# A RetNet layer and a SwiGLU layer on one core: a new order of work, rms_g spread by a product, two row groups transposed by DMA

## Chip, core and metric

One core of one Trainium2 chip. The metric is the device time of one execution in microseconds; each version is run several times and the median counts.

## What is computed

The first half is a recurrent attention with a decaying state, for 4 batches, 8 heads, 768 positions and a head size of 64. The second half normalises each of the 3072 rows of 512, and puts it through a gated layer of width 1536.

```python
for t in range(S):                       # S = 768
    state = gamma * state + k[:, :, t] (outer) v[:, :, t]
    y[:, :, t] = scale * (q[:, :, t] @ state)
x = y.transpose(0, 2, 1, 3).reshape(3072, 512)
xn = x / sqrt(mean(x * x, axis=-1) + 1e-6) * rms_g
g = xn @ w_gate                          # 512 x 1536
out = (g / (1 + exp(-g)) * (xn @ w_val)) @ w_out
```

## The kernel before, in words

The sequence is cut in six chunks (c = 0 to 5) of 128 positions; a chunk has four rows (b = 0 to 3, one for each batch) of 128 positions by 512 columns. Within a chunk the recurrence is done as masked products, and the state carries the rest to the next chunk.

No loop sets the order of work. A string, `ORDER`, lists some 870 steps; each engine runs its own steps strictly in the order of the list, and the waits between engines follow from the data. A step is written name.arguments@engine/banks. The engine letters are D (VectorE), A (ScalarE), P (GpSimd) and S (SyncE, which issues transfers alone). The number behind the slash is one of the eight PSUM banks; a step that writes a bank waits until what was in it has been read.

The steps, with c and b as their first arguments:

- `Lq`, `Lk`, `Lv`: a load of a row of q, k or v (256 KB in float32). GpSimd's loads of q and k turn the values to bfloat16 on the way; rows loaded by SyncE are turned by `Cq` (for c > 0 with a factor) and `Ck`. Loads of chunk 2 wait for the last part of w_out. The buffers are rings (qf, kf: 4, vf: 6, qb: 6, kb: 8).
- `wg`, `wv`, `wo`: a load of some of the twelve 128-wide parts of w_gate, w_val, w_out, all issued by GpSimd.
- `Tq`, `Tk` with `Eq`, `Ek`: a transpose on TensorE into a bank, and its copy to SBUF; from chunk 2 on `tq`, `tk` do both by a DMA transpose, issued by SyncE.
- `A` (scores into two banks a row), `M0`, `M1` (the mask, VectorE), `V` (v times its decay), `Y` (y into a bank), `K` and `U` (the chunk's addition to the state), `B` (state to bfloat16, GpSimd).
- `x` (chunk 1 only, y times its decay), `S` (sum of squares, ScalarE), `R` (1/rms, two GpSimd instructions), `N` (x times 1/rms times rms_g, VectorE).
- `X` with `XE`: the transpose of xn on TensorE and its copy to SBUF; `XE` on SyncE is a DMA transpose in place of both.
- `g`, `v` (c, first and last part, first and last row): gate and value products of the FFN, four matmuls a part; `s` (silu, ScalarE, a ring of 3), `h` (their product, VectorE). In chunk 0 they are cut by rows, so that they can start with the first rows and parts.
- `d`, `e`: the output products, `o` their copy to SBUF (a ring of 4), `st` the store.
- `hot.n`: n matmuls of ones whose result nobody reads. `iota`, `ident`, `causal`: masks made on GpSimd; `vd`, `yd`, `mk0`, `mk1`: decays and masks on ScalarE; `tab`: one silu of one column, which loads ScalarE's table; `rms`: the load of rms_g.

The setup ahead of the list puts a few memsets on VectorE, among them those of the bfloat16 states and of `causal`, which the step `causal` then masks. In the list before, the first steps of GpSimd are `ident`, two loads, `iota`, four loads and parts of the weights; `causal` comes in chunk 0's FFN. `rms` reads rms_g's 512 values once for each of the 128 partitions.

Of the kernel before, what the change touches and what calls it, by code (L numbers as in the profile page):

```python
# [27 lines left out]
g.0.4.5.0.3/4 N.0.3 Ek.1.0@A Tq.1.0/2 wv.9.12 s.0.4.5.0.3 X.0.3/1 Eq.1.0@D K.0.2/0 s.0.5.6.0.3 K.0.1/3 XE.0.3@D
A.1.0/42 g.0.4.6.3.4/5 wv.6.9 M0.1.0 g.0.0.4.3.4/1 U.0.2@A U.0.1@A h.0.5.6.0.3 v.0.4.6.3.4/4 M1.1.0
g.0.8.9.0.4/0 s.0.4.6.3.4 h.0.4.5.0.3 v.0.0.4.3.4/3 s.0.0.4.3.4 Lk.1.1@P g.0.7.8.0.4/7 wg.9.12 V.1.0@D Tk.1.2/2  # L30
g.0.6.7.0.4/5 B.0.2 s.0.8.9.0.4 h.0.4.6.3.4 B.0.1 Y.1.0/6 v.0.11.12.0.4/1 Ek.1.2@A Lq.1.2@P h.0.0.4.3.4 K.1.0/0
# [6 lines left out]
d.0.1.4.8 V.1.2@P M0.1.3 d.0.3.4.8 M0.1.2 V.1.3@P M1.1.3 K.1.2/5 Y.1.2/0 U.1.2@D X.1.1/4 Y.1.3/6 x.1.2 XE.1.1@A
B.1.2 K.1.3/5 d.0.2.4.8 x.1.3 S.1.2 U.1.3@D Lq.2.0@S S.1.3 d.0.0.8.12 R.1.2 Lk.2.0@S d.0.2.8.12 Lv.2.0@S R.1.3
N.1.2 o.0.0@A st.0.0@S d.0.1.8.12 B.1.3 N.1.3 o.0.2@A Lq.2.1@S X.1.2/4 X.1.3/0 o.0.1@A d.0.3.8.12 XE.1.2@D  # L40
Cq.2.0@P XE.1.3@A Lk.2.1@S K.1.1/6 g.1.3.4.0.4/5 o.0.3@A U.1.1@D Ck.2.0@P tq.2.0 v.1.1.2.0.4/3 B.1.1 s.1.3.4.0.4
g.1.0.1.0.4/1 st.0.3@S V.2.0@P st.0.2@S g.1.6.7.0.4/2 s.1.0.1.0.4 Lv.2.1@S tk.2.0 Cq.2.1@P g.1.1.2.0.4/4
s.1.6.7.0.4 v.1.3.4.0.4/0 Lq.2.2@S Ck.2.1@P tq.2.1 g.1.2.3.0.4/7 h.1.3.4.0.4 g.1.9.10.0.4/6 s.1.1.2.0.4 st.0.1@S
h.1.1.2.0.4 tk.2.1 v.1.0.1.0.4/5 g.1.11.12.0.4/1 V.2.1@P Lk.2.2@S h.1.0.1.0.4 v.1.7.8.0.4/2 s.1.2.3.0.4 Lv.2.2@S
v.1.2.3.0.4/0 Cq.2.2@P v.1.6.7.0.4/4 h.1.2.3.0.4 tq.2.2 v.1.8.9.0.4/3 h.1.6.7.0.4 v.1.9.10.0.4/5 Lq.2.3@S
s.1.9.10.0.4 s.1.11.12.0.4 g.1.8.9.0.4/7 Ck.2.2@P h.1.9.10.0.4 Lk.2.3@S g.1.4.5.0.4/0 tk.2.2 s.1.8.9.0.4 V.2.2@P
A.2.0/4615 h.1.8.9.0.4 s.1.4.5.0.4 v.1.10.11.0.4/7 Lv.2.3@S M1.2.1 M0.2.1 K.2.1/3 Cq.2.3@P v.1.5.6.0.4/0 M0.2.0
# [474 lines left out]
```

## Time and profile before

| | |
|---|---|
| median of 3 runs | 239.07 us (238.51 to 240.12) |
| the profiled execution, first to last instruction | 236.7 us |
| last TensorE matmul ends | 233.76 us |
| granted TensorE clock | 1.000 |
| filler matmuls (hot_ps) | 121, 10.7 us busy |
| ScalarE copies, last one ends | 234.06 us |
| data moved | 34.89 MB, mean 147 GB/s |

The profiled execution has no time of its own apart from its span; the median stands 2.4 us above that span. Times in the profile count from the span's start. TensorE's busy time includes the fillers, and the ends of matmuls are modelled.

Rows that are used below, from the views by line and by tile (one instruction each unless said otherwise):

| what | engine | us |
|---|---|---|
| mask on scores, am<-a_ps 128x512 | VectorE | 0.68 |
| silu times value, hT, 128x512 | VectorE | 0.68 |
| x<-y_ps, st_f addition | VectorE | 0.69 |
| xn, 128x512 | VectorE | 0.75 |
| kT, qT, xnT copies, 128x512 bf16 | VectorE / ScalarE | 0.42 / 0.59 |
| kb from kf, 128x512 | GpSimd / ScalarE | 0.61 / 0.62 |
| vp from vf, 128x512 | GpSimd / VectorE / ScalarE (8 parts) | 1.04 / 0.69 / 2.02 |
| qb from qf, 128x512 | GpSimd | 1.04 |
| sum of squares, with the read of its result | ScalarE | 0.80 |
| 1/rms, two instructions | GpSimd | 0.75 |
| table load for silu | ScalarE | 1.28 |
| DMA transpose of xn, issue / issue to landing | SyncE | 1.22 / 2.5 |
| store of a row, issue to landing | SyncE | 2.0 late in the run |

### The profile page before, as it was taken

The numbers are of one execution on the slowest core, as the hardware profiler recorded it, in microseconds if no ns is written. First come the engines' busy times: TensorE is split into PE (matmuls) and PEld (weight loads), VectorE is DVE, ScalarE is ACT, GpSimd is POOL, SyncE is SP. The second block draws the span as 40 slices with busy tenths as digits, with TensorE's granted clock in tenths as the row PEclk, the third lists the DMA queues.
The fourth block names the chain that finished last, engine by engine and source line by source line (L and its number), as shares of the span: only waits on it lengthen the run. The fifth ranks groups of instructions, "written<-read, shape, count | busy, mean of one in ns | idle before, by whom it ended". The sixth has DMA issues, their size and how long they took to land.

```text
span 236.7 us, 4515 instructions
## 1 busy us (share of the span) xinstructions
PE 227.5 (96%) x1729; PEld 123.5 (52%) x1729; DVE 121.1 (51%) x212; ACT 87.7 (37%) x187; POOL 109.5 (46%) x182
## 2 busy tenths in 40 slices
PE   8889999989999999899999999999999999999995
...
GB/s 142 206 208 160 149 206 188 126 209 130 235 231 210 191 195 154 194 248 123 39 233 171 179 204 158 198 138 141 215 216 74 0 25 95 38 47 0 44 44 134
DMA packets 105045, 34.89 MB, mean 147 GB/s; under 512 B 94464, under 2 KB 101504, under 8 KB 105024
## 3 DMA queue, kind: packets, MB, share of 16 engines
...
q10 hardware_dynamic: 144, 0.10, 0.1%
...
HBM read 28.57 MB, written 6.29 MB: 147 GB/s over the span
## 4 chain that ended last, share of the span: by engine, by line
PE 71%; DMA 13%; POOL 6%; DVE 3%; issue 2%; ACT 1%; SPq 1%; POOLq 0%; DVEq 0%; ACTq 0%
PE v_ps L436 22%; PE o_ps L461 21%; PE g_ps L436 21%; DMA vf<-in_v_dram 4%; DMA wo_b<-in_moe_w_out_dram 3%; DMA kb<-in_k_dram 3%; DMA wg_b<-in_moe_w_gate_dram 3%; PE y_ps L353 2%; PE y_ps L357 1%; PE a_ps L335 1%; POOL kb L262 1%; PE kv_ps L413 1%; PE o_ps L483 1%; DVE xn L385 1%; POOL vp L303 1%
## 5 line engine op out<-in xcount | busy, mean ns | idle before, releaser
L454 DVE TENSOR_TENSOR hT<-sg,v_ps 128x512 bf16<-128x512 bf16 (+2 forms) x75 | 48.7, 663 | 63.2 <-ACT sg L446 32.0
L436 PE MATMUL v_ps<-xnT,wv_b 128*128 128x512 bf16 (+2 forms) x328 | 70.9, 353 | 1.2 <-DVE am L343 1.1
L436 PE MATMUL g_ps<-xnT,wg_b 128*128 128x512 bf16 (+2 forms) x328 | 70.8, 353 | 0.4 <-DMA wg_b<-in_moe_w_gate_dram 0.3
L446 ACT ACTIVATE sg<-g_ps 128x512 bf16<-128x512 f32 (+2 forms) x75 | 43.3, 581 | 65.3 <-PE g_ps L436 56.3
L461 PE MATMUL o_ps<-wo_b,hT 128*128 128x512 bf16 x276 | 63.5, 379 | 0.9 <-DMA wo_b<-in_moe_w_out_dram 0.9
L436 PEld LDWEIGHTS <-wv_b 128*128 128x128 bf16 x328 | 29.4, 98 | 30.7 <-DMA xnT<-xn 1.5
L436 PEld LDWEIGHTS <-wg_b 128*128 128x128 bf16 x328 | 29.5, 98 | 29.7 <-DMA wg_b<-in_moe_w_gate_dram 0.5
L461 PEld LDWEIGHTS <-hT 128*128 128x128 bf16 x276 | 26.1, 98 | 29.5 <-issue 0.9
L142 ACT COPY o_sb<-o_ps 128x512 f32<-128x512 f32 (+2 forms) x20 | 11.2, 558 | 45.3 <-PE o_ps L461 41.1
L343 DVE TENSOR_TENSOR am<-a_ps,causal 128x512 bf16<-128x512 f32 x40 | 25.4, 684 | 2.0 <-PE a_ps L335 1.6
L287 POOL TENSOR_TENSOR qb<-qf,ydec 128x512 bf16<-128x512 f32 x16 | 16.7, 1043 | 18.3 <-DMA qf<-in_q_dram 17.9
L303 POOL TENSOR_TENSOR vp<-vf,vdec 128x512 bf16<-128x512 f32 x18 | 18.7, 1043 | 13.2 <-DMA vf<-in_v_dram 13.1
L428 POOL CAST st_b<-st_f 64x256 bf16<-64x256 f32 x40 | 16.7, 417 | 16.6 <-DVE st_f L421 8.6
L385 DVE SCALAR_TENSOR_TENSOR xn<-y_ps,rstd,g_bc 128x512 bf16<-128x512 f32 x20 | 14.9, 750 | 13.0 <-POOL rstd L379 11.8
L371 ACT ACTIVATE xsq<-y_ps 128x512 f32<-128x512 f32 x20 | 11.9, 597 | 14.1 <-PE y_ps L357 12.0
L377 POOL TENSOR_SCALAR ms<-ssq 128x1 f32<-128x1 f32 x24 | 5.1, 214 | 22.7 <-ACT xsq L371 21.3
L142 POOL CAST kb<-kf 128x512 bf16<-128x512 f32 x16 | 9.8, 611 | 10.0 <-DMA kf<-in_k_dram 9.4
L379 POOL TENSOR_TENSOR rstd<-ms,mhalf 128x1 f32<-128x1 f32 x24 | 13.3, 553 | 2.0
L421 DVE TENSOR_TENSOR st_f<-st_f,kv_ps 128x512 f32<-128x512 f32 x16 | 10.8, 683 | 4.6 <-PE kv_ps L413 4.6
L216 PE MATMUL hot_ps<-one 128*128 128x128 bf16 x121 | 10.7, 257 | 1.1 <-DVE one L149 1.1
L353 PEld LDWEIGHTS <-am 128*128 128x128 bf16 x192 | 8.4, 98 | 3.7 <-DVE am L343 0.6
L216 PEld LDWEIGHTS <-one 128*128 128x128 bf16 x121 | 9.4, 119 | 1.6 <-DVE one L149 1.1
...
## 6 DMA issues: line engine op xcount, KB each, us to landing
...
```

What stands on the lines that cost most here:

```text
L142: (e.copy if e is ACT else e.tensor_copy)(out, in_)
L216: nc.tensor.matmul(p, one, one, start=True, stop=True)
L287: e.tensor_tensor(out=u["qb"], in0=u["qf"], in1=ydec[:, c, :, None].to_broadcast([128, H, D]), op=ALU.mult)
L303: e.tensor_tensor(out=u["vp"], in0=u["vf"], in1=vdec[:, c, :, None].to_broadcast([128, H, D]), op=ALU.mult)
L343: DVE.tensor_tensor(out=u["am"][:, i], in0=u["a"][i], in1=m, op=ALU.mult)
L379: POOL.tensor_tensor(out=u["rstd"], in0=ms, in1=mhalf, op=ALU.pow)
L385: DVE.scalar_tensor_tensor(out=u["xn"], in0=flat(u.get("x", u["y"])), scalar=u["rstd"], in1=g_bc, op0=ALU.mult, op1=ALU.mult)
L428: POOL.tensor_copy(st_b[b][r, :, i * 64:i * 64 + 64], st_f[b][r, :, i * 64:i * 64 + 64])
L436: nc.tensor.matmul(p[:, (n - n0) * m:(n - n0 + 1) * m], W[w][0][:, s, n * 128:(n + 1) * 128], xnT[c][:, s, b0 * C:b1 * C], start=s == 0, s ...
L446: ACT.activation(sg[:, :cols], done["wg", c, n0, b0][:, :cols], AF.Silu)
L454: DVE.tensor_tensor(out=hT[c][:, n0:n1, b0 * C:b1 * C], in0=sg, in1=p, op=ALU.mult)
L461: nc.tensor.matmul(o_ps[c, b], hT[c][:, n, b * C:(b + 1) * C], wo_b[:, n, :], start=n == 0, stop=n == NFF - 1)
```

## The change

The list is a new one: 873 steps in place of 877, on all engines and in all chunks, and nearly every step stands in another place. Beside the order, these things differ:

- GpSimd begins with `iota`, `ident` and `causal`, and then issues v of row 0, and the q and k (and v of row 2) of chunk 0's rows, ahead of the first weights. v of row 1 is SyncE's now, and v of row 0 GpSimd's.
- `rms` loads one row of rms_g; `G` multiplies it in float32 by a row of ones into a PSUM bank, which spreads it over the 128 partitions, and `GE` copies the bank to g_bc.
- Rows 0 and 1 of chunk 1 are transposed by DMA (`XE.1.0@S`, `XE.1.1@S`); their `X` steps are gone.
- 90 fillers in place of 121.
- From chunk 2 on, 23 of the conversions that GpSimd did (11 `Ck`, 2 `Cq`, 10 `V`) are on ScalarE or VectorE; some copies `o`, `Eq`, `Ek` trade engines, and two stores go from SyncE to ScalarE.

The diff, the list cut to the places that are spoken of:

```diff
--- before.py
+++ after.py
 ORDER = """
-ident Lq.0.0@S hot.48/0 Lq.0.1@P Lk.0.0@S Lk.0.1@P vd yd iota Lv.0.0@S Lv.0.1@P Lk.0.2@P mk0 Lq.0.2@P Cq.0.0@D
-Ck.0.0@A Lv.0.2@P Tk.0.0/0 Tq.0.0/1 mk1 wg.0.2 hot.8/3 Ek.0.0@D Eq.0.0@D Tq.0.1/2 wv.0.2 V.0.0@D A.0.0/34
-Eq.0.1@A hot.13/0 M0.0.0 rms@S Lv.0.3@P tab M1.0.0 Tk.0.1/5 hot.6/0 Lq.0.3@P Ek.0.1@D Y.0.0/6 V.0.1@D A.0.1/70
-S.0.0 wv.2.4 hot.12/2 M1.0.1 R.0.0 Tk.0.2/1 M0.0.1 hot.8/0 N.0.0 Tq.0.2/2 Ek.0.2@A Y.0.1/3 Eq.0.2@D X.0.0/4
-S.0.1 Lk.0.3@P A.0.2/50 XE.0.0@D hot.19/1 V.0.2@A M1.0.2 R.0.1 M0.0.2 wg.2.4 g.0.0.2.0.1/7 N.0.1 Y.0.2/6 wv.4.6
-s.0.0.2.0.1 X.0.1/1 S.0.2 v.0.0.2.0.1/2 XE.0.1@D R.0.2 g.0.0.2.1.2/4 K.0.0/0 v.0.0.2.1.2/5 s.0.0.2.1.2 N.0.2
-U.0.0@A hot.3/1 h.0.0.2.0.1 X.0.2/3 B.0.0 Tq.0.3/7 V.0.3@A XE.0.2@D hot.4/0 v.0.0.2.2.3/1 wg.4.6 v.0.2.3.0.3/4
...
-wo.0.4 v.0.6.7.0.4/4 x.1.0 v.0.7.8.0.4/2 S.1.0 Tq.1.1/3 v.0.8.9.0.4/6 s.0.6.7.0.4 Eq.1.1@D R.1.0 g.0.11.12.0.4/3
-h.0.8.9.0.4 Lq.1.3@P U.1.0@D Tk.1.1/5 s.0.7.8.0.4 g.0.9.10.0.4/6 N.1.0 Lv.1.1@P g.0.10.11.0.4/0 Ek.1.1@A
-h.0.7.8.0.4 B.1.0 A.1.1/75 s.0.11.12.0.4 K.0.3/2 Lk.1.3@P d.0.0.0.4/3 h.0.11.12.0.4 U.0.3@A M0.1.1 wo.4.8
...
-st.5.0@S e.5.3.1/1 o.5.2@A st.5.2@S d.5.1.10.12 o.5.3.1@D e.5.3.0/6 st.5.3.1@A o.5.1@D st.5.1@S e.5.3.2/2
-o.5.3.0@A st.5.3.0@S o.5.3.2@A st.5.3.2@S
+iota ident Lq.0.0@S mk1 hot.48/7 Lk.0.0@S yd Ck.0.0@A Tk.0.0/7 causal Cq.0.0@D Lv.0.0@P mk0 Lq.0.1@P vd Lk.0.1@P
+Tq.0.0/0 Ek.0.0@D Lv.0.1@S Eq.0.0@D V.0.0@D hot.11/0 A.0.0/45 Lq.0.2@P V.0.1@A rms.1@S Tq.0.1/1 M0.0.0 Lq.0.3@P
+G/3 Lk.0.2@P Tk.0.1/7 M1.0.0 Y.0.0/5 Ek.0.1@A Eq.0.1@D GE@D Tq.0.2/4 S.0.0 A.0.1/71 Lv.0.2@P Eq.0.2@D M1.0.1
+Lk.0.3@P M0.0.1 wg.0.2 Tq.0.3/6 Eq.0.3@D wv.0.2 hot.9/0 Tk.0.2/3 Lq.1.0@P Y.0.1/0 K.0.0/2 R.0.0 V.0.2@D Ek.0.2@A
+S.0.1 N.0.0 A.0.2/46 M0.0.2 K.0.1/3 U.0.0@A M1.0.2 tab Lv.0.3@P hot.12/1 Tk.0.3/5 wg.2.4 X.0.0/7 hot.10/1
+Y.0.2/1 Ek.0.3@A XE.0.0@D R.0.1 N.0.1 S.0.2 A.0.3/72 X.0.1/5 U.0.1@A XE.0.1@A g.0.0.2.0.1/0 Lk.1.0@P K.0.2/3
+wv.2.4 M1.0.3 g.0.0.2.1.2/5 v.0.0.2.1.2/6 v.0.0.2.0.1/4 M0.0.3 s.0.0.2.1.2 R.0.2 N.0.2 V.0.3@D X.0.2/2 Y.0.3/5
+s.0.0.2.0.1 h.0.0.2.1.2 Tq.1.0/0 XE.0.2@A K.0.3/1 h.0.0.2.0.1 wg.4.6 wg.6.9 g.0.0.2.2.3/7 Eq.1.0@D wv.6.9
+s.0.0.2.2.3 S.0.3 U.0.3@A v.0.0.2.2.3/2 h.0.0.2.2.3 g.0.2.3.0.3/4 wv.4.6 Tk.1.0/2 R.0.3 Ek.1.0@D N.0.3
+g.0.3.4.0.3/7 s.0.3.4.0.3 v.0.3.4.0.3/6 A.1.0/70 wg.9.12 U.0.2@A h.0.3.4.0.3 X.0.3/1 B.0.0 g.0.5.6.0.3/5
+XE.0.3@D M1.1.0 g.0.0.4.3.4/2 g.0.4.5.0.3/1 Lq.1.1@P v.0.0.4.3.4/3 v.0.2.3.0.3/0 Lv.1.0@P s.0.0.4.3.4
+g.0.6.7.0.4/2 s.0.2.3.0.3 s.0.6.7.0.4 h.0.2.3.0.3 h.0.0.4.3.4 v.0.6.7.0.4/6 s.0.5.6.0.3 B.0.3 h.0.6.7.0.4
+Lq.1.3@P M0.1.0 g.0.7.8.0.4/0 s.0.4.5.0.3 v.0.4.5.0.3/3 g.0.8.9.0.4/6 s.0.8.9.0.4 v.0.5.6.0.3/2 g.0.4.6.3.4/4
+g.0.10.11.0.4/6 h.0.5.6.0.3 Lk.1.2@P V.1.0@D v.0.4.6.3.4/2 s.0.7.8.0.4 K.1.0/0 h.0.4.5.0.3 Lk.1.1@P
+v.0.8.9.0.4/1 Lk.1.3@P wv.9.12 s.0.4.6.3.4 Lq.1.2@P v.0.7.8.0.4/4 Tq.1.3/5 g.0.9.10.0.4/7 U.1.0@D h.0.4.6.3.4
+h.0.8.9.0.4 Tk.1.3/0 s.0.9.10.0.4 Eq.1.3@D g.0.11.12.0.4/1 wo.0.4 Tk.1.1/2 Tk.1.2/7 Ek.1.3@A h.0.7.8.0.4
+A.1.3/35 s.0.11.12.0.4 Lv.1.1@P Ek.1.2@D Y.1.0/1 M1.1.3 Ek.1.1@A Tq.1.1/4 v.0.11.12.0.4/7 x.1.0 Tq.1.2/1
+Eq.1.1@A M0.1.3 h.0.11.12.0.4 S.1.0 Lv.1.2@P v.0.9.10.0.4/2 wo.4.8 Eq.1.2@A A.1.2/71 Lv.1.3@P B.0.1 M1.1.2
+s.0.10.11.0.4 v.0.10.11.0.4/4 A.1.1/03 M0.1.1 M1.1.1 wo.8.12 d.0.0.0.4/5 V.1.1@P d.0.3.0.4/1 R.1.0 M0.1.2
+Y.1.1/0 x.1.1 V.1.2@D d.0.1.0.4/3 B.0.2 h.0.9.10.0.4 d.0.2.0.4/6 S.1.1 K.1.2/7 R.1.1 Y.1.2/0 N.1.0 K.1.1/2 x.1.2
+N.1.1 d.0.1.4.8 d.0.3.4.8 h.0.10.11.0.4 U.1.2@D d.0.2.4.8 S.1.2 V.1.3@P XE.1.1@S Y.1.3/0 R.1.2 U.1.1@D d.0.0.4.8
+K.1.3/4 Lv.3.1@S d.0.1.8.12 x.1.3 S.1.3 U.1.3@D d.0.0.8.12 d.0.3.8.12 N.1.2 XE.1.0@S o.0.1@A Lk.2.1@S Lq.2.1@S
+Lq.2.3@S R.1.3 Lk.2.0@S N.1.3 X.1.2/7 Cq.2.1@P X.1.3/4 XE.1.2@D d.0.2.8.12 o.0.2@D XE.1.3@A Lq.2.0@S Lv.2.0@S
+g.1.9.10.0.4/7 Ck.2.1@D Cq.2.0@P o.0.3@D Lk.3.1@S g.1.5.6.0.4/4 B.1.0 s.1.9.10.0.4 B.1.3 o.0.0@A g.1.8.9.0.4/7
...
+S.2.2 V.3.1@A M1.2.3 tk.3.1 N.2.0 tq.3.0 d.1.0.0.10/1 Y.2.3/4 d.1.0.10.12 Lk.3.2@S o.1.0@D Lk.5.1@S B.2.0
+d.1.1.0.10/3 R.2.2 S.2.3 o.1.3@A N.2.2 A.3.0/5721 d.1.1.10.12 B.2.1 R.2.3 Ck.3.2@P N.2.3 d.1.2.0.12/0 XE.2.0@S
+M0.3.1 XE.2.1@S XE.2.2@S M1.3.1 XE.2.3@S st.0.0@S Lq.3.3@S Y.3.1/6 K.2.2/2 K.3.1/1 S.3.1 v.2.1.2.0.4/4 o.1.2@D
+g.2.1.2.0.4/0 Lq.4.1@S M0.3.0 s.2.1.2.0.4 U.2.2@D Lq.4.0@S U.3.1@D Lv.4.0@S M1.3.0 Lk.4.0@S g.2.7.8.0.4/2
+Cq.3.2@P Ck.3.3@A g.2.2.3.0.4/7 R.3.1 o.1.1@D g.2.3.4.0.4/0 g.2.9.10.0.4/1 s.2.7.8.0.4 Lv.3.2@S h.2.1.2.0.4
+v.2.2.3.0.4/2 K.2.3/3 s.2.2.3.0.4 N.3.1 V.3.0@A s.2.3.4.0.4 v.2.7.8.0.4/6 v.2.3.4.0.4/7 h.2.2.3.0.4 Cq.3.3@P
+tk.3.2 st.1.0@S g.2.8.9.0.4/0 Lk.4.1@S U.2.3@D tq.3.2 Cq.4.1@P Lv.4.2@S Ck.4.0@D B.2.2 h.2.7.8.0.4 h.2.3.4.0.4
...
+d.4.1.0.10/6 d.4.1.10.12 h.5.2.3.0.4 s.5.10.11.0.4 d.4.0.0.10/1 d.4.0.10.12 o.4.1@D h.5.10.11.0.4 o.4.0@A
+o.4.3@A st.4.1@S st.4.3@S d.5.1.0.10/4 st.4.0@S e.5.3.2/6 d.5.1.10.12 o.5.1@D o.5.3.2@A d.5.0.0.10/7 d.5.0.10.12
+d.4.2.0.12/2 st.5.1@S o.5.0@D e.5.3.0/4 o.5.3.0@A o.4.2@A st.5.3.0@S d.5.2.0.12/7 st.5.3.2@A st.4.2@S st.5.0@A
+e.5.3.1/3 o.5.2@A o.5.3.1@A st.5.2@S st.5.3.1@A
 """
@@ -174,6 +174,9 @@
     mask0 = const.tile([128, 2, NHP, C], F32, name="mask0")
     causal = const.tile([128, 128], BF16, name="causal")
     g_bc = const.tile([128, DM], F32, name="g_bc")
+    g_row = const.tile([1, DM], F32, name="g_row")
+    ones = const.tile([1, 128], F32, name="ones")
+    DVE.memset(ones, 1.0)
     warm = const.tile([128, 1], F32, name="warm")
     st_f = [const.tile([128, NHP, 2 * D], F32, name=f"st_f{b}") for b in range(B)]
     st_b = [const.tile([128, NHP, 2 * D], BF16, name=f"st_b{b}") for b in range(B)]
@@ -250,8 +253,17 @@
         ACT.activation(warm, zero, AF.Silu)
 
     @op
-    def rms(e, bk):
-        e.dma_start(out=g_bc, in_=moe_rms_g.partition_broadcast(128))
+    def rms(e, bk, one_row):
+        e.dma_start(out=g_row, in_=moe_rms_g.partition_broadcast(1))
+
+    @op
+    def G(e, bk):
+        done["G"] = bank(bk[0], [128, DM], F32, "g_row_ps")
+        nc.tensor.matmul(done["G"], ones, g_row, start=True, stop=True)
+
+    @op
+    def GE(e, bk):
+        copy(e, g_bc, done["G"])
 
     def load(n, e, c, b):
         if e is POOL and n != "v":
```

115 lines of the change are left out of this document (46 added, 69 removed).

## The prediction, made before the change was run

> **What bounds the kernel now.** I read the page first, for the share of each engine; then TensorE's waits; then the chain of waits in order of time; then the timeline of GpSimd and TensorE over the first 35 us, which gives every load's issue; and the tile views of the weights and rows, for issue to landing. On the page:
>
> ```profile
> span 236.7 us, 4515 instructions
> PE 227.5 (96%) x1729; PEld 123.5 (52%) x1729; DVE 121.1 (51%) x212; ACT 87.7 (37%) x187; POOL 109.5 (46%) x182
> PE   8889999989999999899999999999999999999995
> ```
>
> TensorE is the bound, and its row is 9 nearly all the way. But "busy" counts filler: the page's group hot_ps is 10.7 us. So I made a ledger: start of each group of matmuls, less the time that the real matmuls ahead of it need at the rate of the dense stretches (chain: 3.45 us for 16 of 128x512, so 0.863 for four; 0.223 for four of 128x128; 0.457 for a y group of 12, 0.234 of 8; 0.276 for one row's eight a_ps; 0.65 for four of 128x384). All real matmuls together are 213.2 us: g and v 124.5, output products 62.2, a_ps 6.6, y_ps 10.1, kv 4.5, transposes 5.3. TensorE ends at 233.8, so 20.5 us are lost. The ledger shows where: 13.0 by the first g product (15.85), 15.9 at 31.65, 17.1 at 51.34, 17.8 at chunk 1's first g (61.18), 19.3 at 98.18, 20.4 at the end. Three quarters go in the first 32 us. The waits name the rest:
>
> ```profile
> PE xt_ps L398 <- DVE xn L385: 1.1, 3, 0.5
> PE v_ps L436 <- DVE am L343: 1.1, 1, 1.1
> PE o_ps L461 <- DMA wo_b<-in_moe_w_out_dram: 0.9, 1, 0.9
> PE g_ps L436 <- DMA wg_b<-in_moe_w_gate_dram: 0.3, 1, 0.3
> ```
>
> What sets the first 32 us is in the chain: a row load of 7.3 us, then GpSimd's issues one behind the other, then a weight load.
>
> ```profile
> 4.91 7.31 DMA kb<-in_k_dram
> 24.47 7.13 DMA wg_b<-in_moe_w_gate_dram
> 43.45 7.85 DMA wo_b<-in_moe_w_out_dram
> ```
>
> And GpSimd's timeline: first load at 1.70, about 0.9 us per row load, 0.8 per weight; its queue waits for rstd, masks and state casts in between (15.37 to 20.17 only two weights go out).
>
> ```profile
> 1.70 1.09 POOL L262 DMA_DIRECT2D qb<-in_q_dram  x1
> 3.67 0.31 POOL L220 TENSOR_SCALAR_AFFINE_SELECT row_f<-row_f 128x128 f32<-128x128 f32 x1
> 7.53 0.79 POOL L271 DMA_DIRECT2D wg_b<-in_moe_w_gate_dram  x1
> 24.47 0.80 POOL L271 DMA_DIRECT2D wg_b<-in_moe_w_gate_dram  x1
> 26.22 0.29 POOL L229 TENSOR_SCALAR_AFFINE_SELECT causal<-causal 128x128 bf16<-128x128 bf16 x1
> ```
>
> **Part 1: GpSimd starts later.** iota, ident and causal now stand ahead of its first load. causal waits for VectorE's memset of the same tile (2.88 to 3.05 now, about 0.06 later for the new memset of ones). So causal ends near 3.4, and the first load goes out at 3.45 instead of 1.70; every load waits behind it. With 0.9 us a load: v row 0 at 3.45, q1 4.4, k1 5.3, q2 6.2, q3 7.1, k2 8.0, v2 8.9, k3 9.8, wg.0.2 10.7, wv.0.2 11.5, q of chunk 1 12.2. To landing I take 4.9 us, as at 20.98 to 23.59 (4.86 to 4.98), where nothing else loaded; the upper bound is the 7.2 of the crowded start, in which SyncE's three rows and the 256 KB broadcast of rms_g (6.8 us) shared the engines. That broadcast is now one row. Landings: q1 9.3 (before 7.3), k1 10.2 (10.0), k2 12.9 (12.2), q3 12.0 (18.2), k3 14.7 (20.1), wg.0.2 16.0 (15.0), wv.0.2 17.3 (16.4).
>
> **Part 2: first FFN product.** Walked along the new TensorE order. The 48 fillers end at 6.4 as now; hot.11 takes bank 0, which Eq.0.0 reads until 7.7, so A.0.0 goes at 8.6 (7.83 now). Tq.0.1 at 9.35, G, then Tk.0.1 at 10.5. G, a float32 product of 512 columns, has no row here: at least one 0.216 us product, at most 1.7 (eight of them). I take 0.9, since it stands in a wait for k1 that hides 0.6 of it; its cost on the path is 0 to 1.1. Y.0.0 10.8, A.0.1 11.6, Tk.0.2 12.9, Y.0.1 13.3, A.0.2 14.0, twelve fillers (0.8), Tk.0.3 15.35, X.0.0 15.6, ten fillers, Y.0.2 16.6. A.0.3 needs Ek.0.3, which on ScalarE stands behind S.0.1 (to 14.8), U.0.0 (15.4) and tab (1.28 + 0.20, to 16.9): 17.55. X.0.1, then the first g at 18.05. Real work ahead of it is 5.4, so lost 12.7, against 13.0 now. Two more waits follow: K.0.2 reuses K.0.1's bank, which ScalarE frees by U.0.1 at 18.9, and XE.0.1 behind it (19.5): 0.9 us. X.0.2, Y.0.3, X.0.3 meet their inputs within 0.2. With a few tenths of such waits the ledger is 14.2 at K.1.0, near 36.
>
> Weights no longer cut this stretch. R.0.3 waits for S.0.3 until 23.8 on GpSimd, and wg.9.12, B.0.0 and all chunk 1's loads queue behind it, yet: wg.4.6 lands 24.2 (needed 25.8), wg.6.9 26.3 (29.6), wv.6.9 28.3 (30.5), wv.4.6 29.6 (32.2), wg.9.12 31.5 (35.0), wv.9.12 38.6 (41.9), wo.0.4 42.6 (45.5), wo.4.8 47.2 (50). The increments are 1.3 us per 512 KB read, 2.0 per 768 KB, 3.2 per 1 MB, 0.85 per row load, as landings follow each other now. Cover is about 2 us each; gone, the excess is lost in full. The 0.9 us for wo goes: its third part is issued near 39 instead of 46.83.
>
> **Part 3: chunk 1's transposes.** X.1.0 and X.1.1 go (2 x 0.223 off TensorE); in their place two SyncE transposes, 1.22 us issue each and 2.5 to landing. N.1.1 is done near 52.1, so XE.1.1 lands 54.6 and XE.1.0 about 57, Lv.3.1 and chunk 2's loads queued between and behind; chunk 1's first g comes at 58.5. Covered by 1.5. The two rows that TensorE still transposes: Y.1.3 ends 53.5; x, S, R, N (0.69, 0.8, 0.75, 0.75, plus U.1.3 and N.1.2 ahead) give 56.95; X.1.3 stands at 57.4. So the 1.1 us of xn waits go, and I add 0.5 for bank waits at A.1.2 and Y.1.1. Ledger 14.7 at chunk 1's first g, 17.8 before: 3.1 gained, 0.45 given back since the new real work is 213.7 (G 0.9 more, X 0.45 less).
>
> **Part 4: the dense part, chunks 1 to 5.** Before it loses 2.6 after 61 us, 1.2 of it at 98.18, where only 4.0 us of work lay between the end of Y.2.3 and the first chunk 2 product. The new order has 7.1 there (8.3 and 8.7 for chunks 3 and 4): XE.2.3 lands about 1.7 ahead, so the 1.2 goes. Against it, g.2.2.3 needs the bank that M1.3.0 frees, behind o.1.2, U.2.2 and U.3.1 on VectorE, and g.2.10.11 that of s.2.11.12: 0.4 together. Dense loss 1.8, range 0.8 to 4.
>
> **Part 5: the end.** Last store now: issued at 234.09, 0.33 after TensorE, landed 1.57 later, span end 1.04 after that: 2.94. New: the last product is a 192-column piece, copy 0.32, then a store on ScalarE's queue that takes 1.72 (as the one at 232.09): 3.1.
>
> **Sum:** 213.7 + 14.7 + 1.8 + 3.1 = 233.3 of span against 236.7, so -3.4. The median of 239.07 stands 2.4 above the span; kept, that gives 235.7.
>
> **A rule against it.** Fillers fall from 121 to 90. Trace: the first 48 fillers start 107 ns apart (5.30 us), those after 7.04 about 55. The Trainium skill, "TensorE: Matmul & The Clock Gate", "What you observe" and "HAM oscillation", has the array run at half rate by default and fall back after some 3.4 us of idleness; the trace agrees with the first half. My longest idle stretch in the new order is 1.0 us (now 1.03), so by that rule nothing happens.
>
> **Rivals.** (a) *The rows are not early.* The list puts q and k first, but GpSimd starts 1.75 late and k1, k2, wg.0.2 land later than now. If landings take 7.2 rather than 4.9, first g moves to about 20.4, ledger 15.0; with the 0.9 and 0.6 that follow it above and the weights 2.3 later, which uses up their cover and costs some 0.6 at two places, chunk 1 starts at the 17.8 of before: 213.7 + 17.8 + 1.8 + 3.1 + 2.4 = 238.8, no change. For: the crowded start's 7.2. Against: loads that caused it are fewer. (b) *VectorE and ScalarE take over the waits for loads.* 23 conversions of chunks 2 to 5 (11 of k, 2 of q, 10 of v) leave GpSimd, which waited on qf 17.9 us, vf 13.1 and kf 9.4 in 23 waits, 1.8 each, at no cost. On the new engines h and s stand behind, which free the banks. A bank comes round with 1 to 2 us to spare; it decides when a wait outlasts that. If five of 23 outlast it by 1.5: 7.5 us, 243.2, slower. For: several margins are under 0.2. Against: most rows are loaded a chunk ahead (chunk 2 from 55 us, used from 73). (c) *The clock falls* in the thinner start: real work (5.4) and 42 fillers (2.3) at half rate cost up to 7.7 before the waits, I say 3.5 on the path: 239.2.
>
> **How the numbers follow.** Forecast 0.56 (233.0 to 238; 0.46 of it under 236.7), (a) 0.19, (b) 0.20, (c) 0.05. One per cent, 2.4 us, is about what can be told from no change. Faster 0.48: 0.46, and 0.02 from (a). Same 0.29: 0.10, 0.14 of (a), 0.04 of (c), 0.01 of (b). Slower 0.23: 0.19 of (b), 0.03 of (a), 0.01 of (c). Range 232.8 to 242: down to a dense loss of 0.8 and a start 1.9 better, up to most of (b). Forecast's own range 233.0 to 238.
>
> **What would show it.** First load at 3.4 on GpSimd; first g at 18, ledger 12.7; no TensorE wait for weights or wo; chunk 1's first g at 58.5; at chunk 2's first v no stop. Wrong if wg or wv weights appear among TensorE's waits, if VectorE waits for kf or vf show up with TensorE behind them, or if fillers after 7 us run at 107 ns.

## The result, and the profile after

| | before | after |
|---|---|---|
| median, us | 238.79 (237.79 to 240.12, 4 runs) | 248.12 (247.25 to 249.16, 4 runs) |
| profiled execution: its time / its span, us | – / 236.7 | 247.29 / 245.3 |

The change makes the kernel slower: ratio 1.0387, 95% interval [1.0319, 1.0454]. The forecast was 235.7. The median of before has one run more than the table ahead of the prediction.

On the page of the changed kernel, the first line, the line of engines, TensorE's row of 40 slices and the row of its granted clock:

```profile
span 245.3 us, 4474 instructions
PE 229.3 (93%) x1692; PEld 123.0 (50%) x1692; DVE 131.1 (53%) x229; ACT 94.9 (39%) x235; POOL 91.9 (37%) x159
PE   7799999999979997698899599999999999999995
PEclk9979999999999999999999799999999999999999
```

A slice is 6.1 us. TensorE's row has dents at 67 to 74, 92 to 104 and 135 to 141 us, where before it was 9 or 8; the clock is lower in two slices, the third (from 12 us) and the 23rd (from 135 us). Its longest waits (line, what was waited for, us in all, times, longest):

```profile
PE g_ps L448 <- DMA xnT<-xn: 2.6, 1, 2.6
PE v_ps L448 <- DMA xnT<-xn: 2.0, 1, 2.0
PE a_ps L347 <- DMA qT<-qb: 1.8, 2, 1.6
PE v_ps L448 <- ACT sg L458: 1.3, 1, 1.3
PE g_ps L448 <- ACT sg L458: 1.2, 1, 1.2
```

The waits of before for weights and w_out are gone. In their place stand waits for what SyncE issues, normalised rows (xnT, 4.6 us) and transposed q (1.8), and two waits for a bank that ScalarE's silu frees (2.5). The ledger of the prediction, at the first feed-forward matmul of each chunk (start in us, and in brackets the us lost up to there), with four of the experiments:

| kernel | chunk 1 | chunk 2 | chunk 3 | chunk 4 | end |
|---|---|---|---|---|---|
| before | 61.18 (17.8) | 98.18 (19.3) | 132.31 (19.6) | 168.89 (20.3) | (20.4) |
| after | 58.59 (14.8) | 100.68 (20.9) | 138.05 (26.2) | 166.06 (28.1) | (28.4) |
| e1_new_start | 59.17 (15.3) | 99.47 (20.2) | 135.02 (21.8) | 172.43 (23.3) | (23.5) |
| e13_new_start_queue_first | 59.35 (15.5) | 96.72 (17.4) | 132.07 (18.9) | 169.18 (20.1) | (20.2) |
| e17_after_queue_mended_4 | 59.09 (15.3) | 99.18 (19.4) | 134.96 (23.1) | 164.56 (26.6) | (30.6) |
| e18_queue_and_scores | 59.07 (15.2) | 98.85 (19.1) | 134.61 (22.8) | 162.08 (24.1) | (25.1) |

In some traces (e1 and e18 here) 25 of TensorE's 1,692 matmul records are missing; there the steps were matched to the records by their kind, in order.

The start won 3.0 us, where 3.1 were forecast. Chunk 1 gave them all back and more (6.1 us lost), chunk 2 lost another 5.3. What led there is in the chain of waits, between 91 and 101 us and ahead of chunk 3 (start, us, what):

```profile
91.46 2.42 DMA qT<-qb
...
94.01 0.62 PE a_ps L347 x16
94.63 3.14 PE o_ps L473 x14
97.80 0.32 DVE o_sb L142
98.12 2.42 DMA xnT<-xn
...
135.58 2.42 DMA xnT<-xn
```

A DMA transpose is issued, 2.42 us later it has landed and TensorE starts. The question is why it was issued no sooner. SyncE's own timeline, around chunk 2's rows (start, us of issue, form, number):

```profile
90.13 1.21 SPq L331 DMA_TRANSPOSE kT<-kb  x1
91.46 1.21 SPq L331 DMA_TRANSPOSE qT<-qb  x1
92.72 1.21 SPq L274 DMA_DIRECT2D kf<-in_k_dram  x2
94.02 5.31 SPq L416 DMA_TRANSPOSE xnT<-xn  x4
99.39 0.57 SPq L486 DMA_DIRECT2D out_dram<-o_sb  x1
100.01 2.05 SPq L274 DMA_DIRECT2D qf<-in_q_dram  x3
```

A load takes SyncE some 0.57 us to issue and a DMA transpose 1.22, one after the other. From 55.2 to 138 us it issues 30 transposes, 39 loads and 8 stores, for 76.5 us of these 83; at 1.22 and 0.57 us each they would take 63, so some 13 are issues that took longer, which the views don't tell apart from waits. In the kernel before, the same queue issues 75 in that time for 72.4 us, with one long gap, 3.8 us from 111.5, ahead of a normalised row.

What the queue does to the rows can be read directly. Chunk 3's last row is normalised by 130.34 us; SyncE turns to it at 135.58, behind a load, a transpose for a later chunk, another row and a store (VectorE's line, then SyncE's):

```profile
129.60 0.74 DVE L397 SCALAR_TENSOR_TENSOR xn<-y_ps,rstd,g_bc 128x512 bf16<-128x512 f32 x1
...
131.59 0.58 SPq L274 DMA_DIRECT2D qf<-in_q_dram  x1
132.28 1.26 SPq L331 DMA_TRANSPOSE qT<-qb  x1
133.64 1.22 SPq L416 DMA_TRANSPOSE xnT<-xn  x1
134.91 0.58 SPq L486 DMA_DIRECT2D out_dram<-o_sb  x1
135.58 1.23 SPq L416 DMA_TRANSPOSE xnT<-xn  x1
```

The same two steps of the kernel before:

```profile
126.96 0.75 DVE L385 SCALAR_TENSOR_TENSOR xn<-y_ps,rstd,g_bc 128x512 bf16<-128x512 f32 x1 [0.72 <-POOL rstd L379]
...
129.75 1.22 SPq L404 DMA_TRANSPOSE xnT<-xn  x1
```

From the end of its normalisation to its issue the last row waits 3.1 us in chunk 2 and 5.2 in chunk 3 (before 1.5 and 2.0); the longest wait of any row is 9.4 and 19.3 us (before 1.5 and 2.0).

The new list loads further ahead: between a load of chunks 2 to 5 and the transpose of that row (for v, its conversion) lie on average 14.1 places of SyncE's queue (up to 34), before 5.8. Counted from the lists, ahead of the last normalised row of chunk 2 the queue holds 10 loads and 4 transposes for later chunks (6 and 4 before), of chunk 3 14 and 6 (6 and 4 before). And the two rows of chunk 1 that now go by DMA head it: it waits for the first of them until 52.3 (not until 53.5, as two expectations below have it), and the first load of chunk 2 goes out at 55.62 us, no sooner than before (55.28).

The theories tested: **Q**, SyncE's queue, one issue after the other, paces the dense part, either by its order (Qo) or because TensorE's new order asks sooner than it can give in any order (Qd); **C**, rival (b) of the prediction, VectorE and ScalarE wait for loads with the conversions that GpSimd had; **D**, the throughput of the DMA engines; **T**, TensorE's order gives the gain back by itself.

### The profile page after: what moved, and what is told of

It reads as the page before. It is cut to its first block, busy times and chain, and to the rows that moved or that the text cites. A ratio compares the mean times of both kernels' runs of the same rounds, so it can differ in the third digit from the quotient of the medians.

```text
span 245.3 us, 4474 instructions
## 1 busy us (share of the span) xinstructions
PE 229.3 (93%) x1692; PEld 123.0 (50%) x1692; DVE 131.1 (53%) x229; ACT 94.9 (39%) x235; POOL 91.9 (37%) x159
## 4 chain that ended last, share of the span: by engine, by line
PE 65%; DMA 13%; DVE 7%; ACT 5%; POOL 4%; SPq 3%; issue 2%; POOLq 0%; DVEq 0%; ACTq 0%
PE g_ps L448 20%; PE v_ps L448 19%; PE o_ps L473 18%; PE a_ps L347 2%; DMA kf<-in_k_dram 2%; DMA qf<-in_q_dram 2%; DMA vf<-in_v_dram 2%; DMA qT<-qb 2%; DMA xnT<-xn 2%; DMA qb<-in_q_dram 2%; SPq L274 2%; DVE hT L466 2%; DVE am L355 1%; DMA kT<-kb 1%; PE y_ps L365 1%
## 5 line engine op out<-in xcount | busy, mean ns | idle before, releaser
L448 PE MATMUL v_ps<-xnT,wv_b 128*128 128x512 bf16 (+2 forms) x328 | 71.8, 356 | 3.3 <-DMA xnT<-xn 2.0
L458 ACT ACTIVATE sg<-g_ps 128x512 bf16<-128x512 f32 (+2 forms) x75 | 41.6, 577 | 76.2 <-PE g_ps L448 63.5
L473 PEld LDWEIGHTS <-hT 128*128 128x128 bf16 x276 | 26.2, 98 | 29.2
L355 DVE TENSOR_TENSOR am<-a_ps,causal 128x512 bf16<-128x512 f32 x40 | 26.2, 683 | 5.8 <-PE a_ps L347 5.7
L299 POOL TENSOR_TENSOR qb<-qf,ydec 128x512 bf16<-128x512 f32 x14 | 15.5, 1106 | 24.1 <-DMA qf<-in_q_dram 23.8
L397 DVE SCALAR_TENSOR_TENSOR xn<-y_ps,rstd,g_bc 128x512 bf16<-128x512 f32 x20 | 14.8, 747 | 10.9 <-POOL rstd L391 10.7
L313 ACT ACTIVATE vp<-vf,vdec 128x64 bf16<-128x64 f32 x64 | 16.1, 336 | 4.0 <-DMA vf<-in_v_dram 4.0
L142 ACT COPY o_sb<-o_ps 128x512 f32<-128x512 f32 (+2 forms) x14 | 7.1, 522 | 27.2 <-PE o_ps L473 16.9
L142 DVE COPY o_sb<-o_ps 128x512 f32<-128x512 f32 x12 | 8.2, 689 | 17.1 <-PE o_ps L473 16.1
L391 POOL TENSOR_TENSOR rstd<-ms,mhalf 128x1 f32<-128x1 f32 x24 | 14.0, 582 | 2.0
L315 POOL TENSOR_TENSOR vp<-vf,vdec 128x512 bf16<-128x512 f32 x8 | 8.3, 1039 | 11.2 <-DMA vf<-in_v_dram 11.0
L347 PE MATMUL a_ps<-qT,kT 64*128 64x128 bf16 x192 | 8.6, 221 | 2.3 <-DMA qT<-qb 1.8
L433 DVE TENSOR_TENSOR st_f<-st_f,kv_ps 128x512 f32<-128x512 f32 x16 | 10.7, 677 | 0.1
```

Of the source, the lines that this page charges most:

```text
L142: (e.copy if e is ACT else e.tensor_copy)(out, in_)
L299: e.tensor_tensor(out=u["qb"], in0=u["qf"], in1=ydec[:, c, :, None].to_broadcast([128, H, D]), op=ALU.mult)
L313: ACT.activation(u["vp"][:, h], u["vf"][:, h], AF.Copy, scale=vdec[:, c, h:h + 1])
L347: nc.tensor.matmul(u["a"][i][:, hp, :], u["kT"][r, hp, :], u["qT"][r, hp, :], start=True, stop=True)
L355: DVE.tensor_tensor(out=u["am"][:, i], in0=u["a"][i], in1=m, op=ALU.mult)
L391: POOL.tensor_tensor(out=u["rstd"], in0=ms, in1=mhalf, op=ALU.pow)
```

## The experiments

Each edit is of the list; times are medians, beside a ratio to the kernel before run on the same chip.

**1. The halves of the list apart.** The new list up to chunk 1's first feed-forward matmul, then the old one, and the reverse.

```diff
 # e1_new_start: new start without its loads of chunks >= 2
-(old list up to g.1.3.4.0.4)
+(new list up to g.1.9.10.0.4)
 # e2_new_dense
-(old list from g.1.3.4.0.4 on)
+(new list from g.1.9.10.0.4 on)
```

> The new list up to chunk 1's first gate product (without the loads of later chunks in it), then the old list for the rest. Theory Q (the dense part loses because SyncE's queue, which issues one transfer after another from 55 us on without a pause, carries its transfers in a worse order): the new start keeps its gain, the old dense part its old loss: 213.7 + 14.6 + 2.6 + 2.9 = 233.8 of span, about 236 us. Theory C (the 23 conversions moved to VectorE and ScalarE wait for loads there): the same, 236. If the new start were the cause (loads of chunk 2 that start late), it would stay near 247.

> The old list up to chunk 1's first gate product, then the new list. Theories Q and C: the old start's ledger of 17.8 and the new dense part's loss of 13.6 add up: 213.2 + 17.8 + 13.6 + 3.1 = 247.7 of span, about 250 us. If the start were the cause: 239.

Measured: 240.67, 1.004 [1.0005, 1.0075], and 249.56, 1.0389 [1.0336, 1.0441]. The whole loss lies in the new dense part. But the new start alone gains nothing, where both theories expected 236: its chunk 1 begins 2.0 us sooner than before, its chunk 2 1.3 us later. There SyncE's loads of chunk 2 begin at 55.00 us, before at 55.28: the start is earlier, the supply is not.

**2. Conversions, and the queue's load.** On the changed list, 23 conversions of chunks 2 to 5 back to GpSimd; and 16 loads of v issued by GpSimd rather than SyncE.

```diff
-Ck.2.1@D V.3.1@A ...
+Ck.2.1@P V.3.1@P ...      # e3_conv_pool
-Lv.2.0@S Lv.2.1@S ...
+Lv.2.0@P Lv.2.1@P ...      # e4_v_loads_pool
```

> The new list, with the 23 conversions of chunks 2 to 5 back on GpSimd. Theory C: the waits for loads leave VectorE and ScalarE, most of the 11 us of extra dense loss goes: 237 to 239 us. Theory Q: SyncE's order is as before, its transposes come as late: 243 to 250 us.

> The new list, with the 16 loads of v of chunks 2 to 5 issued by GpSimd in place of SyncE. Theory Q: some 0.75 us of SyncE's queue for each, 9 of them by 138 us, so its transposes come up to 7 us earlier and more than half of the stops of TensorE go: 239 to 243 us. Theory O (the order of TensorE's and VectorE's steps with its tight banks loses by itself, whatever the transfers): 246 to 248 us.

Measured: 248.79, 1.0349 [1.0278, 1.042]: C falls as the cause of the loss; with the conversions gone from VectorE and ScalarE the waits are for kT 2.6, qT 2.5 and xnT 3.2 us. And 243.87, 1.0131 [1.005, 1.0212]: the same bytes with 16 issues fewer on SyncE take back 2.6 of the 3.9 per cent; the time lies between Q's range and O's. Chunk 2's first matmul comes at 98.36 there, chunk 3's at 134.24; the profiled execution took 248.69 us, 4.8 above the median, and what it loses more lies behind 145 us, so only these two times of that trace are used.

**3. More load on the old list.** The kernel before, with a small DMA more behind each of the 16 loads of v on SyncE.

```diff
         if c == 2:
             after(i, ("wo", 8))
+        if n == "v" and c >= 2:
+            SP.dma_start(out=ring([16, D], F32, "pad", 16), in_=rows["q"][b, c][:16, 0])
```

> The kernel before with 16 more DMAs on SyncE's queue, one behind each load of v of chunks 2 to 5, of 16 partitions x 256 bytes into a buffer that nobody reads: SyncE's issue time grows by 16 times some 0.5 us, the bytes by 64 KB in all (0.2%). Q: SyncE's queue is full from 55 to 140 us already, where 10 of the 16 lie, so 3 to 6 us slower: 242.5 to 247. D: within 0.7 us of before. T: within 0.7 us of before.

Measured: 245.56, 1.0166 [1.0084, 1.0247]. The 16 issues took 0.57 to 2.53 us each, median 0.87. Six of them lie ahead of chunk 2's last rows, 4.45 us together, and from chunk 1's first matmul to chunk 2's the ledger loses 4.6 us, before 1.5. With 0.2% more bytes, D can't make that: the old list, too, has no room left on SyncE. Nor do transfers take longer once issued: the median from issue to landing of a normalised row's transpose is 2.5 us before, 2.5 in the changed kernel and 2.4 here. TensorE's waits show it in the same forms as the change does:

```profile
PE v_ps L438 <- DMA xnT<-xn: 2.3, 2, 1.6
PE a_ps L337 <- DMA kT<-kb: 1.8, 2, 1.5
```

The Trainium skill, "DMA: Bandwidth & Descriptors", "Issuing engines are not separate DMA queues", says that issuing on several engines saves only the time on the sequencer, usually small beside the transfer. Here that time, 0.57 us for a load that takes 3.4 us to land, adds up over 77 issues to most of 83 us.

**4. An earlier supply for the new start.** New start, old dense part, with SyncE's stream moved forward in three ways.

```diff
 # e5_start_early_queue, against e1
-XE.1.1@S XE.1.0@S
+X.1.0/7 XE.1.0@A X.1.1/2 XE.1.1@A
 # e6_start_v_pool: e5, and
-Lv.2.0@S Lv.2.1@S ...
+Lv.2.0@P Lv.2.1@P ...
 # e9_queue_first, against e1
-XE.1.1@S XE.1.0@S Lq.2.0@S Lk.2.0@S Lv.2.0@S st.0.0@S Lq.2.1@S Lk.2.1@S tq.2.0 st.0.3@S st.0.2@S
+Lk.2.0@S Lq.2.0@S Lk.2.1@S Lq.2.1@S XE.1.1@S XE.1.0@S Lv.2.0@S tk.2.0 Lq.2.2@S tq.2.0
 # e13_new_start_queue_first, against e9
-Ck.2.0@P R.1.3
+R.1.3 Ck.2.0@P
```

> The new start and the old dense part, as in the run before that gave 240.7 us, but the normalised rows 0 and 1 of chunk 1 are transposed by TensorE again, and so SyncE's queue does not begin with two DMA transposes that wait for those rows until 53.5 us; chunk 2's loads can be issued as soon as the last third of the output weights has landed, at about 50.8 us rather than 55.0. If SyncE's queue paces the dense part (Q), the whole stream is some 3 us earlier: 237 to 238.5 us. If the DMA engines' throughput paces it (D), the stream also starts earlier, but what it has to move is the same: 238 to 240. If the start's gain is lost to the order of TensorE's work itself (T), 240.5 to 241.5 (the eight transposes are added).

> As the run beside it (new start, old dense part, rows 0 and 1 by TensorE), and the 16 loads of v for chunks 2 to 5 are issued by GpSimd. Same bytes, 16 issues of about 0.55 us fewer for SyncE. Q: another 1 to 2 us off, 235.5 to 237.5, the best of all so far. D: the same time as the run beside it, within 0.5 us. T: no change either; and if GpSimd, which converts q and k in the old dense part, becomes late by the issuing, slower than the run beside it.

> The new start and the old dense part again, now with SyncE's stream really earlier: in the runs before it could not move, first because two DMA transposes waiting until 53.5 us headed it, then because the store of chunk 0's row 0 stood fifth and waited until 60.5 us. Here k and q of chunk 2's rows 0 and 1 head the queue (from 50.8 us, when the output weights have landed), then the two transposes, then chunk 2 as in the list before, with chunk 0's four stores behind the first transposes of q and k; GpSimd converts row 0's k before it handles the last row of chunk 1. Q (the queue supplies the dense part at its own pace, and a start's gain counts only if the supply starts earlier too): the 3 us come through to the end, 236.5 to 238.5 us. D (DMA throughput): 239 to 240.5. T (TensorE's order gives the gain back by itself): 240.5 to 241.5.

> The run with chunk 2's rows at the head of SyncE's queue and the old dense part (0.993 of before) with one step put back: GpSimd converts row 0's k behind chunk 1's last row rather than ahead of it, since in that run the last row waited for it and the first matmul of chunk 1's feed-forward came at 60.7 rather than 59.2 us. Q: first matmul at 59 to 59.5, and up to 1.5 us off the whole, ratio 0.985 to 0.993. If the supply and not TensorE sets that part: 0.991 to 0.996.

Measured: e5 241.53, 1.0105 [1.0058, 1.0152], nearest to T's 240.5 to 241.5. The queue did not get free: three loads went out from 50.8 us on, but the store of chunk 0's row 0 stood next and waited for its data until 60.5, with everything else behind it. e6 245.39, 1.0172 [1.0089, 1.0255], slower than any theory said: GpSimd issued each load of v only when it had done its conversion of the one before, so the waits went there. Its chain of waits, between 67 and 83 us:

```profile
67.40 4.79 DMA vf<-in_v_dram
...
72.26 0.99 POOL vp L312
73.24 4.27 DMA vf<-in_v_dram
...
77.58 0.98 POOL vp L312
78.56 4.65 DMA vf<-in_v_dram
```

e9, where chunk 2's loads do go out first, 239.03, 0.9929 [0.9888, 0.9969]; e13 238.99, 1.0008 [0.9962, 1.0053]. e9 misses Q's range and lies in D's, which e4 and e8 speak against; e13's ratio lies above both of its ranges. In absolute times both are 1.6 to 2.5 us below e1 and e5, and chunk 2 begins at 97.1 and 96.7 us, the earliest of all kernels (e1 99.5, before 98.2). So an earlier supply lets part of the gain through, as far as chunk 2. But e13, 1.8 us ahead of the kernel before at chunk 1, is 1.5 ahead at chunk 2, 0.2 at chunk 3 and 0.3 behind at chunk 4: there the lead is given back, and whether by the queue or, as T says, by TensorE's order, no run shows. The times of e9 and e13, which differ in one step, are the same; the ratios differ by the runs of before beside them. No version was shown to beat the kernel before by as much as 1%.

**5. The queue's order on the changed list.** Four attempts to put what is needed next ahead.

```diff
 # e7_loads_later: 30 loads, each to stand 6 to 11 places ahead of its use
 # e10_after_relieved: e4, and
-XE.1.1@S Lv.3.1@P XE.1.0@S Lk.2.1@S Lq.2.1@S Lq.2.3@S Lk.2.0@S Lq.2.0@S Lk.3.1@S
+Lk.2.1@S Lq.2.1@S Lk.2.0@S Lq.2.0@S XE.1.1@S XE.1.0@S
 # e11_before_queue_order: loads, conversions, tq and tk of chunks 2 to 5 in the old list's order
 # e12_after_queue_mended: behind XE.2.3
+Lk.3.2@S Lq.3.2@S Lk.3.3@S
 # and behind XE.3.2
+Lv.4.2@S ... Lk.5.1@S Lq.5.2@S ... Lk.5.0@S ... tk.5.1 tq.5.2
```

> The changed list, with 30 loads of chunks 2 to 5 (and their conversions) moved later in the list, so that each stands 6 to 11 places of SyncE's queue ahead of its first use; in the changed list the mean is 14.1 places with up to 34, in the list of before 5.8. Nothing else is touched. Q: what is needed next is no longer queued behind what is needed later, and most of the 9 us comes back: 239 to 243. D: bytes and their number are the same, so the loss stays: 246 to 249. If the two DMA transposes more at 52 us are the cause: 245 to 248.

> The changed list with two reliefs at once: the 16 loads of v of chunks 2 to 5 issued by GpSimd (alone they gave 243.9 us), and k, q of chunk 2's rows 0 and 1 ahead of the two DMA transposes at the head of SyncE's stream (50.8 rather than 55.6 us), three loads that are needed much later moved back. Q: the two add up, 239.5 to 242.5. D: as with the v loads alone, 243 to 245, or as the changed list, 248. T: the changed list's time, 247 to 249.

> The changed list with the loads, conversions (all on GpSimd) and DMA transposes of q, k, v of chunks 2 to 5 in the order of the list before, each placed by the TensorE work that stands ahead of it; TensorE's order, the rows' transposes and the stores are the changed list's. This parts the two halves of Q. If the order in the queue is at fault (Qo), 239 to 242. If the changed list's TensorE asks for the same rows 3 us (start) and a further 2 to 20 us (order) sooner than the queue can give them in any order (Qd), 244 to 249.

> The changed list with only what stands ahead of the normalised rows in SyncE's queue mended. Counted from the lists: ahead of chunk 2's last row the list before issues 6 loads and 4 transposes for later chunks (8.3 us at 0.57 and 1.22 us each), the changed list 10 and 4 (10.6 us); ahead of chunk 3's last row 6 and 4 (8.3 us) against 14 and 6 (15.3 us). Here the surplus that TensorE's order does not yet ask for stands behind those rows: 6 and 4 at chunk 2, 10 and 4 (10.6 us) at chunk 3; eight loads with their conversions and two transposes are moved, nothing else. Qo: about 2.3 us back at chunk 2's first matmul (100.7 us in the changed kernel) and 4 to 7 us in all at chunk 3's first (138.0 us), so 241 to 244.5. Qd or D: 247 to 249, and the first matmuls of chunks 2 and 3 within 1 us of the changed kernel's.

Measured: 253.42, 1.0484 [1.0413, 1.0555]; 248.21, 1.0306 [1.019, 1.0421]; 263.2, 1.0936 [1.0833, 1.104]; 250.7, 1.0475 [1.0376, 1.0575]. All four miss what Qo said of the time; e10 gives what T said, and e7, e11 and e12 are slower than any theory said. e7 delays rows of its own: TensorE waits 2.5 us for vp at 124 us and 4.2 for qT at 150. In e10 GpSimd issues v only behind a row's statistics, and ScalarE's conversion and silu wait for it (119 us); it does not fit with e4, from which it differs in three loads' places and the head of the queue, and takes much of e4's weight away as a proof of Q. In e11 the normalised rows stand in the queue behind transposes that wait for GpSimd's conversions (xnT: 16.9 us of waits). e12 is the one that moves what the count named (it also puts two of chunk 5's conversions on GpSimd): the last rows of chunks 2 and 3 wait 0.5 and 1.3 us in the queue, not 3.1 and 5.2, chunk 2's first matmul comes at 98.82, 1.9 us sooner (2.3 were counted), chunk 3's at 135.51, 2.5 sooner (4 to 7 were counted); and then one wait costs more than both:

```profile
PE a_ps L343 <- DMA qT<-qb: 6.0, 1, 6.0
```

The loads put back for chunk 5 stood ahead of that transpose.

**6. Following the wait.** Each run mends the place where the one before it lost most.

```diff
 # e15_after_queue_mended_2: chunk 4's last transposes ahead of chunk 5's loads
+XE.3.2@S Lv.4.2@S tk.4.2 tq.4.2 Lv.4.3@S tk.4.3 tq.4.3 Lq.5.1@S Lq.5.3@S Lk.5.3@S ...
 # e16_after_queue_mended_3
-XE.2.3@S ... st.0.0@S    Cq.5.1@D Ck.5.3@D
+st.0.0@S XE.2.0@S ...    Cq.5.1@P Ck.5.3@P
 # e17_after_queue_mended_4: GpSimd handles chunk 4's statistics ahead of three conversions (and SyncE's tq.5.1 and tk.5.2 later)
+R.4.0 R.4.1 ... Cq.5.1@P ... R.4.2 R.4.3 Ck.5.2@P Cq.5.0@P
 # e18_queue_and_scores: SyncE's queue, and TensorE's A.5.0
-tk.5.1 tq.5.2 tk.5.0 Lk.5.2@S XE.4.1@S XE.4.3@S XE.4.2@S
+XE.4.1@S tk.5.1 Lk.5.2@S XE.4.3@S XE.4.2@S tk.5.0 tq.5.0 tq.5.2
-A.5.0/5461 K.4.2/0 v.4.3.4.0.4/2 d.3.0.0.10/3 d.3.0.10.12
+K.4.2/0 v.4.3.4.0.4/2 d.3.0.0.10/3 d.3.0.10.12 A.5.0/5461
```

> The run with the mended queue (chunk 2's first matmul at 98.8 rather than 100.7 us, but 250.7 us in all, since there the loads moved back for chunk 5 stood ahead of the transposes of chunk 4's rows 2 and 3, and TensorE waited 6.0 us for one of them) with that mended too: those four transposes stand directly behind chunk 3's last normalised row, chunk 5's seven loads behind them, and four conversions for which VectorE and ScalarE waited are on GpSimd. If what stands ahead in SyncE's queue sets each wait (Qo), the 6 us go, and 1 to 2 us of waits for VectorE and ScalarE: 242 to 245. If TensorE's order in the changed list asks for more than the queue can give in any order (Qd), the wait turns up at the next row instead: 247 to 251.

> The twice mended run (249.1 us) lost its time at two places that the mending itself made: at 105 us VectorE's eviction of an output row waited for the store of chunk 0's row 0, which stood behind loads in SyncE's queue (landed 105.2), and at 143 us VectorE's conversion of q of chunk 5's row 1 waited for its load (landed 144.4); each time TensorE waited 2 to 3.3 us for the product behind it on VectorE, and then ran some 1.5 us longer at a granted clock of 0.5. Here that store stands ahead of chunk 2's normalised rows, and the two conversions of chunk 5 that VectorE had are GpSimd's. Qo: 2.0 + 3.3 us of waits and two half-clock phases of 1.5 us go, 241 to 243.5. If the list has no slack whatever the order (Qd): 246 to 249, with the wait at a third place.

> The thrice mended run (251.1 us) stood at a ledger of 23.3 us at the scores of chunk 4's rows 2 and 3 (the changed kernel there: 28.1, before: 19.8), and lost 8.5 us behind it at two places: at 144 and at 162 us GpSimd handled the statistics of chunk 4's rows behind conversions of chunk 5 that waited for their loads (landed 143.7 and 161.9), VectorE waited for those statistics (4.0 and 8.3 us), and TensorE for the products behind them. Here those three conversions stand behind chunk 4's statistics. Qo: the ledger at the end is 23.5 to 25.5 and the time 242 to 245 us, most of the 9 us taken back without touching TensorE's order. Qd: 247 to 251, a fourth place.

> The fourfold mended run (249.6 us) had a ledger of 22.9 us from 120 us on (the changed kernel: 23 to 28) and lost it at 161 us: chunk 4's last three normalised rows, ready at 154.5 to 156, stood in SyncE's queue behind three transposes and a load of chunk 5 and were issued at 159.4 to 162; TensorE waited 3.2 and 0.9 us and ran at a granted clock of 0.5 behind it. Those four cannot simply go behind, because the changed list asks for chunk 5's first scores 0.9 us of TensorE work after chunk 4's first matmul. So here both sides move: chunk 4's rows ahead in the queue, and chunk 5's first scores 3.7 us of TensorE work later (behind the output product of chunk 3's row 0), as the one change to TensorE's order. If queue and asking order together make the waits: the wait at 161 us goes, the ledger ends at 23 to 25, the time is 242.5 to 245.5 us. If not, a fifth place, 247 to 250.

Measured: 249.13, 1.0386 [1.0306, 1.0466]; 251.09, 1.043 [1.0324, 1.0535]; 249.61, 1.0378 [1.03, 1.0455]; then 244.08, 1.0178 [1.011, 1.0245]. In the first three the mended wait went each time, another came in its place (a store and a conversion in e15, the statistics of chunk 4 in e16, its normalised rows in e17), and the time stayed. In e17 VectorE has two of chunk 4's rows ready at 155.9, and SyncE still issues two transposes and a load for chunk 5 before it turns to them:

```profile
154.46 1.41 DVE L393 SCALAR_TENSOR_TENSOR xn<-y_ps,rstd,g_bc 128x512 bf16<-128x512 f32 x2 [0.86 <-POOL rstd L387]
```

```profile
155.02 1.22 SPq L327 DMA_TRANSPOSE qT<-qb  x1
156.29 2.36 SPq L327 DMA_TRANSPOSE kT<-kb  x1
158.70 0.57 SPq L270 DMA_DIRECT2D kf<-in_k_dram  x1
159.38 3.84 SPq L412 DMA_TRANSPOSE xnT<-xn  x3
```

By the list neither can go behind: it asks for chunk 5's scores 0.9 us of work after chunk 4's first matmul. Where both sides are moved, e18, the last two rows are issued from 158.17 on, chunk 4 begins 2.5 us sooner than in e17, the granted clock is 1.000 throughout, the ledger ends at 25.1, not 30.6, and the time is in the range that was expected. So there the order of the queue and the order in which TensorE asks make the wait together, as far as this goes: no run moved TensorE's order alone. 3.3 of the 8.0 us by which the changed kernel's ledger is above that of before are taken back, and 4 us of time. The rest is not mended: of the 9.9 us that e18 loses from chunk 1's first feed-forward matmul on, 7.6 go in chunks 1 and 2, where its longest waits are 2.0 us behind VectorE's hT, 1.4 behind ScalarE's silu and 1.1 for a normalised row. 8 of the 23 conversions are back on GpSimd in it; no run has the mended queue and all 23 there.

**7. The half clock.** 40 fillers where TensorE stood idle ahead of chunk 3 in the changed kernel.

```diff
+hot.40/3 g.3.10.11.0.4/3
```

> The changed list with 40 filler matmuls of 128x128 ahead of chunk 3's first matmul, on the bank that it takes, where TensorE stood idle for 2.6 us and the granted clock was 0.5 from 137.8 to 141.2. If the idle time alone makes the clock fall, it stays at 1.0 there and about 1.1 to 1.7 us come back (246 to 247.5 us); if not, the half clock stays and the time is 247.5 to 249.

A single run: 250.7 us, outside both ranges. In it, the last row of chunk 3 took 4.3 us to land instead of 2.4, TensorE was idle for 3.2 us behind the fillers, and the clock fell to 0.5 again, for 6.8 us. The cost of the half clock isn't settled by it.

## Why the prediction was wrong

- *Part 1, GpSimd starts later*: right. First load at 3.59 (3.45 forecast); q1, k1, q3, k3 at 8.7, 9.6, 12.1, 14.6 (9.3, 10.2, 12.0, 14.7); wg.0.2 and wv.0.2 at 17.1 and 18.5 (16.0, 17.3). The 4.9 us to landing were read from rows "where nothing else loaded"; two weight loads were under way there (landed 23.75 and 25.04). Here q1 to k3 took 3.8 to 4.7 us, wg.0.2 6.1.
- *Part 2, first FFN product*: right. First g at 18.38, ledger 13.0 (18.05, 12.7); G is two matmul records and 1.05 us to the next step (0.9); no wait for weights or w_out. Rival (a) fell with it.
- *Part 3*: right as far as it goes. Chunk 1's first g at 58.59, ledger 14.8 (58.5, 14.7). That the two transposes, with "Lv.3.1 and chunk 2's loads queued between and behind", cost nothing later is where it stopped too early: in the changed kernel chunk 2's first load goes out at 55.62 us though w_out has landed at 50.76, and e1, e5 and e9 show that the two transposes and a store hold back the supply of chunk 2.
- *Part 4, the dense part*: the step that failed. "Dense loss 1.8, range 0.8 to 4" was 13.6. "XE.2.3 lands about 1.7 ahead" came from the TensorE work between the last y and the first product, 7.1 us, which left 5.4 for the row; it took 10.7. Y.2.3 ends at 89.80, the row is normalised by 95.02 (5.2 us, behind a conversion of v on ScalarE that leaves the sums late), issued at 98.12 (3.1 us in the queue, behind three other rows) and landed at 100.54, with TensorE waiting 2.0 us. So the step counted what TensorE asks and not what SyncE can issue: some 0.57 us a load and 1.22 a transpose, in order, in a queue that had no room before (e8), whose order the new list made worse (e12: 1.9 us at chunk 2) while asking sooner (e18). The bank waits, 0.4 for two, were mis-sized too: g.2.10.11 alone waited 1.2 us. "Most rows are loaded a chunk ahead", said against rival (b), did not keep ScalarE and VectorE from waiting 11.2 us for loads of k and v between 60 and 170 us.
- *Part 5*: right, 3.0 us from TensorE's last matmul to the end.
- *Rival (b)* had the sign, and 243.2; its mechanism fell as the cause of the loss (e3), but it was there: VectorE's conversion of a row of k waited until 71.13 for a load that SyncE had issued at 68.10, behind two transposes; the silu behind it was late, and TensorE waited 1.3 us, to 73.03, for the bank that it frees, near the 1.5 that (b) gave each such wait. In all, TensorE waits 2.5 us behind ScalarE in the changed kernel, and in-order waits of this kind cost more in e10, e15 and e16.
- *Rival (c)*: the clock did fall, not where it was feared to cost. At 11.5 to 14.9 us little came of it: the ledger at the first product is 13.0, as before, and 12.7 was forecast; at 137.8 to 141.2 the ledger lost some 1.5 us, and that was a consequence of a wait.
- *The signs of being wrong*: three came. TensorE stopped at chunk 2's first v, VectorE's waits for kf stood ahead of a wait of TensorE, and nine fillers from 12.5 us on ran at 107 ns.

Not settled: how the 9 us divide between the order of the queue, the order of asking and the waits on VectorE and ScalarE, and why e10 lost what e4 had won.
